# Head pairs in one TensorE visit, and q transposed like k, in a retention and two-MoE kernel

## The chip, the cores and the metric

The kernel runs on one core of a Trainium2 chip. The metric is device time in microseconds, the median of three runs.

## The reference

Three stages follow each other. All inputs are float32; attention has batch 4, 8 heads, 576 tokens and head dimension 64, and the two feed-forward stages see 2304 tokens of 512 features.

```python
scores = scale * np.matmul(q, k.transpose(0, 1, 3, 2))
gamma = 1.0 - 2.0 ** (-5.0 - np.arange(H))
Dmat = np.where(rel >= 0, gamma[:, None, None] ** rel, 0.0)     # rel = i - j
x = np.matmul(scores * Dmat, v)                                 # then (B*S, H*D)
...
h = np.maximum(np.maximum(x @ w1, x @ w2), x @ w3)              # 512 x 768 each
x = h @ w_out                                                   # 768 x 512
...
g = x @ w_gate                                                  # 512 x 1536
out = (g * sigmoid(g) * (x @ w_val)) @ w_out2                   # 1536 x 512
```

## The kernel before

**Attention in chunks.** Heads are taken in pairs, because two heads of 64 fill the 128 partitions, and tokens in halves of 288, each three chunks of 96. A *unit* is one batch, one head pair and one half, so there are 32 units; unit n belongs to pair n // 2, and even units are first halves. Within a chunk the decay mask is applied to the scores; between chunks a running 64x64 state per head carries what came before. For a unit the code has four steps: `a_prep` (k scaled on GpSimd, k and q brought into transposed form, q scaled by powers of gamma), `a_state` (state matmuls on TensorE, then the chain of states on VectorE), `a_score` (score matmuls, then the mask on VectorE into `pT`), and `a_value` (state times q and `pT` times v into one bank, evicted as a high part `xh` and a low part `xl`).

**Two ways to transpose.** For the first PT = 12 units TensorE transposes k against the identity `ident` (L225) and multiplies q by the diagonal tables `dia` (L228), which transposes and scales it in one; GpSimd makes these tables at the start, and ScalarE copies both results out (L230). From unit 12 on, k and q come from HBM as a 32x32-blocked copy `qk` (`t_load`, L188: eight loads of 72 KB for a pair, in runs of 32 floats), and VectorE transposes the blocks.

**The first feed-forward stage is cut into slices.** `f_slice` takes 288 tokens and 128 columns of one of w1, w2, w3: four blocks of 128 rows, each times three matmuls (high times high and two cross terms). The result of w1 is evicted by ScalarE (L362), those of w2 and w3 are joined to it with a maximum on VectorE (L364). Two PSUM banks alternate, so a slice waits for the eviction of the one two before it. Slices of a batch are queued when its four pairs are done and are spread over the later visits.

**Weights.** The 18 weight tiles of that stage, here weights 0 to 17, are 512 KB of 8-byte floats each, loaded on SP's queue (L106; the names `w` and `w64e` are two buffer pools). `conv_steps` brings one to float32 and splits it: two ScalarE steps (L115, L121), VectorE (L123 to L126), a ScalarE copy (L134) and a GpSimd subtraction (L136). When its fourth step is reached, the load of the weight four further on is issued.

**The order.** `tc.manual_schedule` fixes it: every engine and every queue runs its instructions in the order in which the code is written. `visit(n, slices, convs)` writes one unit's part: the value of unit n, loads for later pairs, states and scores of unit n + 1, then `slices` weight slices, with `a_prep(n + 2)` and the steps of `convs` weight conversions spread between them. The main loop (L505) gives visits 0 to 7 no slices, 8 to 13 four, 14 and 15 six, and later ones five. Until slices exist, `spin` matmuls on zeros stand between visits. After the last unit come the rest of the slices and the other two stages.

Of the kernel before, what the change touches and what calls it, by code (L numbers as in the profile page):

```python
# [41 lines left out]
O_E = O_KS + NP * 2  # L42
O_Q = O_E + NP
O_S = O_Q + H
O_M = O_S + H
# [4 lines left out]
def _constants():  # L50

    c = np.zeros((P, NCONST), np.float64)
    gam = 1.0 - 2.0 ** (-5.0 - np.arange(H))
    j = np.arange(CK)
    c[:CK, O_ID:O_KS] = np.eye(CK)
    c[:CK, O_M:O_G] = j[None, :] >= j[:, None]
    for pr in range(NP):
        for e in range(2):
            g = gam[2 * pr + e]
            c[:CK, O_S + 2 * pr + e] = g ** -j / np.sqrt(D)  # L60
            c[64 * e:64 * e + 64, O_G + pr * CK:O_G + (pr + 1) * CK] = g ** j
            c[:CK, O_KS + 2 * pr + e] = g ** (CK - j) / np.sqrt(D)
            c[64 * e:64 * e + 64, O_E + pr] = g ** CK
            c[:CK, O_Q + 2 * pr + e] = g ** j
    return c.astype(np.float32)
# [3 lines left out]
def retention_moe(ctx, tc, consts, q, k, v, w1, w2, w3, w_out, w_gate, w_val, w_out2, out):  # L69
# [3 lines left out]
    def f(ap):  # L73
        return ap.bitcast(F32)
# [11 lines left out]
    psa = psa_cm.__enter__()  # L86

    cst_a = att.tile([P, O_G], F32, name="cst_a", tag="cst_a", bufs=1)
# [3 lines left out]
    e_t = cst_a[:, O_E:O_Q]  # L92
    q_t = cst_a[0:CK, O_Q:O_S]
    s_t = cst_a[0:CK, O_S:O_M]
    mask = cst_a[0:CK, O_M:O_G]
    g_t = cst_g.rearrange("p (r m) -> p r m", r=NP)
    dia = [att.tile([CK, 2, CK], F32, name=f"dia{i}", tag=f"dia{i}", bufs=1) for i in range(NP)]
    d_t = [att.tile([CK, 2, CK], F32, name=f"dm{i}", tag=f"dm{i}", bufs=1) for i in range(NP)]
# [109 lines left out]
    def a_prep(n):  # L208
# [9 lines left out]
        pool.tensor_tensor(u["ks"][:, 0:nk], u["k"][:, 0:nk], sc, ALU.mult)  # L218
        kq = att.tile([P, 2, C], F32, name="kq", tag="kq", bufs=3)
        kt, qg = kq[:, 0], kq[:, 1].rearrange("p (c m) -> p c m", c=NC)  # L220
        g = g_t[:, pr].unsqueeze(1).to_broadcast([P, NC, CK])
        if n < PT:
            tp = psa.tile([P, 2, 512], F32, name="tp", tag="tp")
            for c in range(NC):
                pe.transpose(tp[:, 0, c * CK:(c + 1) * CK], u["k"][:, c].rearrange("p h d -> p (h d)"), ident)  # L225
            for c in range(NC):
# [50 lines left out]
    def a_value(n):  # L277
# [16 lines left out]
        return lambda: dve.tensor_tensor(xl, o, f(xh), ALU.subtract)  # L294


    w_in = {}
# [83 lines left out]

    def visit(n, slices, convs):
        plan = list(conv_plan(convs))
        done = 0

        def share(j):
            nonlocal done
            upto = len(plan) * (j + 1) // (slices + 1)
# [4 lines left out]
            if n >= 16:  # L393
                for _ in range(1 if j % 2 else 2):
                    next(early, None)

        low = a_value(n)
# [8 lines left out]
        a_state(n + 1)  # L406
        low()
        a_score(n + 1)
        for j in range(slices + 1):
            if j == min(2, slices - 1) or not slices:  # L410
                a_prep(n + 2)
            if j or not slices:
                share(j)
            if j < slices:
                f_some(1)

# [57 lines left out]
    a_load(0, "k", 2)  # L474
    a_load(0, "q", 2, act)
    a_load(0, "v")

    def tables(pr):
        for t, sc, src in ((dia, q_t, ident), (d_t, s_t, mask)):
            pool.tensor_tensor(t[pr], src.unsqueeze(1).to_broadcast([CK, 2, CK]),  # L480
                               sc[:, 2 * pr:2 * pr + 2].unsqueeze(2).to_broadcast([CK, 2, CK]), ALU.mult)

# [11 lines left out]
    spin(1)  # L494
    for n in range(NU):
        if n < NP - 1:
            tables(n + 1)
        if 2 <= n < 6:
            win_load(n - 2)
        if n == 5:  # L500
            win_phase(0, 0)
            win_phase(0, 1)
        if n == 9:
            sp.dma_start(out=cst_g, in_=consts[:, O_G:NCONST])
        visit(n, *((0, 0) if n < 5 else (0, 1) if n < 8 else (4, 2) if n < 13 else (4, 3) if n < 14 else (6, 2) if n < 16 else (5, 0)))  # L505
        if n < 8:
            spin(1)
        if n == 15:
            ask(1)
# [412 lines left out]
```

## Time and profile before

| | us |
|---|---|
| runs | 833.75, 836.33, 833.35 |
| median | 833.75 |
| profiled execution | 833.75 |
| its span in the trace | 831.6 |

The page gives, for each engine, its busy time and share of the span, then the span in 40 equal slices of 20.8 us, each digit a busy share in tenths. The granted clock of TensorE stands at its full level in all 40 slices. The timeline gives instructions in order of their start; consecutive ones of the same form are one row with their count, and where an engine had been idle, the row ends with how long and what ended the wait. TensorE's rows overlap, so the distance between two starts is what a piece of work takes there. The list of DMA issues gives the time from issue to landing.

### The profile page before, as it was taken

How to read it: one execution, taken by the hardware profiler on the slowest of the kernel's cores; microseconds unless marked ns; L12 is line 12 of the kernel's file. 1: busy time of each engine (PE TensorE's matmuls, PEld its weight loads, DVE VectorE, ACT ScalarE, POOL GpSimd, SP SyncE). 2: the span in 40 equal slices, each digit the busy share in tenths (PEclk: the TensorE clock that was granted, in tenths of full speed). 3: DMA queues.
4: the chain of work that ended last, by engine and by line, in shares of the span. 5: the costliest groups of instructions: out<-in, count | busy, mean ns of one | idle time of the engine just before them, and what ended most of it. 6: DMA issues, size and time to landing. Idle time of an engine off the chain costs nothing.

```text
span 831.6 us, 15514 instructions
## 1 busy us (share of the span) xinstructions
PE 817.6 (98%) x5933; PEld 762.7 (92%) x5933; DVE 563.4 (68%) x1007; ACT 315.0 (38%) x633; POOL 208.7 (25%) x194
## 2 busy tenths in 40 slices
PE   9999999999999999999999999999999999999998
PEld 6799899998989999999988999999998999999996
DVE  2678857787874354476587888888899455555554
ACT  3554523333321233565445553444443222332220
POOL 4243320000000002342023333233332333222331
PEclk9999999999999999999999999999999999999999
DMA  9999849999981223865555444334420716565522
GB/s 177 230 202 235 174 119 243 254 251 239 253 225 61 81 99 99 247 180 157 198 207 191 146 159 165 143 137 165 161 80 13 266 49 243 216 226 213 204 92 76
DMA packets 165801, 142.94 MB, mean 172 GB/s; under 512 B 101344, under 2 KB 137952, under 8 KB 165728
## 3 DMA queue, kind: packets, MB, share of 16 engines
q1 hardware_dynamic: 164368, 141.56, 57.7%
q8 instruction: 46, 0.75, 0.4%
q10 hardware_dynamic: 1360, 0.41, 0.2%
q14 instruction: 27, 0.22, 0.1%
HBM read 93.70 MB, written 48.23 MB: 171 GB/s over the span
## 4 chain that ended last, share of the span: by engine, by line
PE 68%; issue 14%; DVE 7%; POOL 6%; ACT 2%; DMA 1%; SPq 1%; POOLq 0%; ACTq 0%; DVEq 0%
PE ps L358 26%; PE g L786 17%; PE ps L763 11%; PE ps L715 6%; POOL gl L834 3%; PE s L248 2%; PE o_ps L289 2%; POOL p L807 2%; PE o_ps L285 2%; PE m_ps L264 1%; SPq L188 1%; PE tp L228 1%; PE psz L380 1%; DMA w<-in_moe_w_val_dram 1%; DVE wz L124 0%
## 5 line engine op out<-in xcount | busy, mean ns | idle before, releaser
L358 PE MATMUL ps<-xl,wh 128*128 128x288 f32 x576 | 173.1, 300 | 3.7 <-DVE hmax L364 3.1
L358 PE MATMUL ps<-xh,wh 128*128 128x288 f32 x576 | 169.7, 295 | 0.0
L358 PE MATMUL ps<-xh,wlo 128*128 128x288 f32 x576 | 169.6, 294 | 0.0
L834 POOL TENSOR_TENSOR gl<-p,gh 128x384 fp32r<-128x384 f32 x72 | 85.8, 1209 | 293.7 <-ACT gh L833 293.7
L763 PE MATMUL ps<-wp,gh 128*128 128x512 f32 (+1 forms) x436 | 135.3, 391 | 0.4 <-DVE acc L768 0.3
L358 PEld LDWEIGHTS ps<-xl,wh 128*128 128x128 f32 x576 | 108.0, 188 | 7.6 <-DVE hmax L364 4.0
L358 PEld LDWEIGHTS ps<-xh,wh 128*128 128x128 f32 x576 | 108.1, 188 | 0.0
L358 PEld LDWEIGHTS ps<-xh,wlo 128*128 128x128 f32 x576 | 108.1, 188 | 0.0
L763 PEld LDWEIGHTS ps<-wp,gh 128*128 128x128 f32 x436 | 80.7, 188 | 14.4 <-DVE acc L768 1.0
L364 DVE TENSOR_TENSOR hmax<-ps,hmax 128x288 f32<-128x288 f32 x96 | 43.6, 455 | 68.6 <-PE ps L358 61.9
L763 PE MATMUL ps<-wp,gl 128*128 128x512 f32 (+1 forms) x218 | 85.6, 393 | 0.0
L768 DVE TENSOR_TENSOR acc<-ps,acc 128x512 f32<-128x512 f32 (+1 forms) x91 | 62.2, 684 | 33.6 <-PE ps L763 31.6
L786 PE MATMUL g<-xhB,wa 128*128 128x384 f32 x288 | 73.4, 336 | 0.0
L786 PE MATMUL g<-xhT,wc 128*128 128x384 f32 x288 | 73.2, 335 | 0.0
L546 POOL TENSOR_TENSOR hl<-hf,hh 128x384 fp32r<-128x384 f32 x26 | 30.0, 1163 | 129.3 <-DMA h_d<-hmax 77.4
L833 ACT ACTIVATE gh<-p 128x384 fp32r<-128x384 f32 x72 | 37.8, 525 | 60.4 <-DVE p L837 53.2
L822 ACT ACTIVATE sb<-u 128x384 f32<-128x384 f32 x36 | 18.9, 525 | 110.0 <-DVE u L820 110.0
L218 POOL TENSOR_TENSOR ks<-kn,cst_a 96x384 f32<-96x384 f32 (+1 forms) x32 | 26.3, 825 | 126.1 <-PE m_ps L264 107.6
L786 PEld LDWEIGHTS g<-xhB,wa 128*128 128x128 f32 x288 | 52.1, 188 | 0.0
L786 PEld LDWEIGHTS g<-xhT,wc 128*128 128x128 f32 x288 | 52.0, 188 | 0.0
L814 DVE TENSOR_TENSOR p<-g,p 128x384 f32<-128x384 f32 x36 | 19.9, 554 | 46.4 <-PE g L786 40.6
L362 ACT ACTIVATE hmax<-ps 128x288 f32<-128x288 f32 x48 | 19.7, 410 | 81.4 <-PE ps L358 81.2
(119 smaller groups left out, 1710.9 us busy)
## 6 DMA issues: line engine op xcount, KB each, us to landing
w<-in_moe_w_out_dram SPq DMA_DIRECT2D x18, 512.0 KB, 4.1
w<-l_d SPq DMA_DIRECT2D x28, 256.0 KB, 2.9
h_d<-hmax SPq DMA_DIRECT2D x48, 144.0 KB, 3.3
w<-in_moe_w_dram SPq DMA_DIRECT2D x12, 512.0 KB, 5.9
w<-in_moe_w_gate_dram SPq DMA_DIRECT2D x12, 512.0 KB, 5.8
w<-in_moe_w_val_dram SPq DMA_DIRECT2D x12, 512.0 KB, 6.0
vn<-in_v_dram SPq DMA_DIRECT2D x16, 288.0 KB, 7.6
out_dram<-acc SPq DMA_DIRECT2D x17, 256.0 KB, 2.0
```

Of the source, the lines that this page charges most:

```text
L218: pool.tensor_tensor(u["ks"][:, 0:nk], u["k"][:, 0:nk], sc, ALU.mult)
L358: pe.matmul(ps, l[:, ksl], r, start=n == 0, stop=n == 3 * KD - 1)
L362: act.activation(mx[hb], ps, ACTF.Copy)
L364: dve.tensor_tensor(mx[hb], ps, mx[hb], ALU.max)
L546: (dve if fi in (3, 5) and hx else pool).tensor_tensor(hl, hf, f(hh), ALU.subtract)
L715: pe.matmul(ps[:, 0:HT], l[:, es], rr, start=n == 0, stop=n == 3 * F1 - 1)
L763: pe.matmul(ps[:, cs], l[:, sl], r[:, cs], start=n == 0, stop=n == 3 * GRP - 1)
L768: dve.tensor_tensor(a[:, cs], ps[:, cs], a[:, cs], ALU.add)
L786: pe.matmul(ps, l[:, ks], r[:, kc], start=first and n == 0, stop=n == 5, skip_group_check=True)
L814: dve.tensor_tensor(p5, g2, p5, ALU.add)
L833: act.activation(gh[half], t, ACTF.Copy)
L834: pool.tensor_tensor(gl[half], t, f(gh[half]), ALU.subtract)
```

## The change

Units 0 to 11 keep single visits. Their q is now transposed on TensorE with three instructions of the form that k has; ScalarE copies only k, and VectorE multiplies q by the table `g` on its way out of PSUM. The `dia` tables and their constants are gone, and the table `cst_g` is loaded at the start on ScalarE's queue instead of at visit 9 on SP's.

From unit 12 on, a visit takes a pair, both halves at once. `pair_value` makes both values in a two-bank tile, with all state matmuls ahead of all `pT` matmuls. `pair_next` makes the states and then the scores of both halves of the next pair in a four-bank tile, the states in columns that the scores leave free. What VectorE and ScalarE do with them is returned as a list of three pieces, which are written ahead of the next slices. The PSUM pool of the first units is closed and a new one opened in visit 11. Pair 6 gets eight slices with five conversions, pair 7 twelve with four, the others ten. `t_load` for pairs 6 to 9 stands in visits 8 to 11 (before: in every other visit, one pair each), and `visit_pair(6)` calls it for pair 9 once more.

```diff
@@ a_prep
-        kq = att.tile([P, 2, C], F32, name="kq", tag="kq", bufs=3)
+        kq = att.tile([P, 2, C], F32, name="kq", tag="kq", bufs=4)
...
-                pe.transpose(tp[:, 0, c * CK:(c + 1) * CK], u["k"][:, c].rearrange("p h d -> p (h d)"), ident)
-            for c in range(NC):
-                for e in range(2):
-                    pe.matmul(tp[64 * e:64 * e + 64, 1, c * CK:(c + 1) * CK], u["q"][:, c, e],
-                              dia[pr][:, e], start=True, stop=True)
-            act.activation(kq, tp[:, :, 0:C], ACTF.Copy)
+            for i, nm in enumerate("kq"):
+                for c in range(NC):
+                    pe.transpose(tp[:, i, c * CK:(c + 1) * CK], u[nm][:, c].rearrange("p h d -> p (h d)"), ident)
+            act.activation(kt, tp[:, 0, 0:C], ACTF.Copy)
+            dve.tensor_tensor(qg, tp[:, 1, 0:C].rearrange("p (c m) -> p c m", c=NC), g, ALU.mult)
@@ new functions
+    def pair_value(j):
+        o = psa.tile([P, 2, 512], F32, name="o_ps", tag="o2")
+        us = [U.pop(2 * j + h) for h in range(2)]
+        for h, u in enumerate(us):
+            for c in range(1 - h, NC):
+                for e in range(2):
+                    hd = slice(64 * e, 64 * e + 64)
+                    pe.matmul(o[hd, h, c * CK:(c + 1) * CK], u["st"][hd, h * NC + c], u["qg"][hd, c],
+                              start=c == 1 - h, stop=False, skip_group_check=True)
+        for h, u in enumerate(us):
...
+                    pe.matmul(o[64 * e:64 * e + 64, h, c * CK:(c + 1) * CK], u["v"][:, c, e], u["pT"][:, e, c],
+                              start=False, stop=True, skip_group_check=True)
...
+            act.activation(xh, o[:, h, 0:C], ACTF.Copy)
...
+            dve.tensor_tensor(xl, o[:, h, 0:C], f(xh), ALU.subtract)
+    def pair_next(j):
...
+        s = psa.tile([P, 4, 512], F32, name="s", tag="s4")
+        m = [s[:, h, C + c * D:C + (c + 1) * D] for h in range(2) for c in range(NC - h)]
...
+        return [chain_states, lambda: weigh(0), lambda: weigh(1)]
@@ visit
-        else:
-            t_load(n // 2 + 2)
+        if n >= PT - 4:
+            t_load(n - 2)
...
+        if n + 1 < PT:
+            a_score(n + 1)
+            late = []
+        else:
+            swap_banks()
+            late = pair_next(PT // 2)
+        ahead = [n + 2] if n < PT - 2 else [PT, PT + 1] if n < PT - 1 else [PT + 2, PT + 3]
...
+    def visit_pair(j, slices, convs):
+        share = sharing(min(slices, 8 if convs else slices), convs, j >= 8)
+        pair_value(j)
+        share(0)
+        a_load(j + 3)
+        t_load(j + 3)
...
+        late = pair_next(j + 1)
+        for x in range(slices + 1):
+            if late:
+                late.pop(0)()
+            if x in (3, 5):
+                a_prep(2 * j + 4 + (x == 5))
+            if x:
+                share(x)
+            if x < slices:
                 f_some(1)
@@ start and main loop
+    act.dma_start(out=cst_g, in_=consts[:, O_G:NCONST])
...
-    for n in range(NU):
+    for n in range(PT):
...
-        if n == 9:
-            sp.dma_start(out=cst_g, in_=consts[:, O_G:NCONST])
-        visit(n, *((0, 0) if n < 5 else (0, 1) if n < 8 else (4, 2) if n < 13 else (4, 3) if n < 14 else (6, 2) if n < 16 else (5, 0)))
+        visit(n, *((0, 0) if n < 5 else (0, 1) if n < 8 else (4, 2)))
...
+    for j in range(PT // 2, NU // 2):
+        visit_pair(j, *((8, 5) if j == 6 else (12, 4) if j == 7 else (10, 0)))
```

The instructions move at three places. In the rows below a row is an instruction with its line, its output, its input and its shape; names of tiles end in a number that is only theirs. First TensorE, before, from the end of one slice to the start of the next in a first half's visit: the value of this unit (`o_ps`), then states (`m_ps`) and scores (`s`) of the next. An f32 matmul of these forms is two passes in the trace.

```order
L358 MATMUL ps<-xh,wh 128x288
L285 MATMUL o_ps<-kq,st 64x96 x4
L289 MATMUL o_ps<-pT,vn 64x96 x6
L264 MATMUL m_ps<-vn,ks 64x64 x4
L248 MATMUL s<-kq 96x96 x6
L358 MATMUL ps<-xl,wh 128x288
```

TensorE after the change, at a pair's visit, where the states share the tile `s` with the scores:

```order
L417 MATMUL ps<-xh,wh 128x288
L304 MATMUL o_ps<-kq,st 64x96 x10
L309 MATMUL o_ps<-pT,vn 64x96 x12
L332 MATMUL s<-vn,ks 64x64 x10
L339 MATMUL s<-kq 96x96 x12
L417 MATMUL ps<-xl,wh 128x288
```

The same four groups stand between two slices, each as long as those of both halves together, and there are half as many such places. Second, SP's queue before the change, from weight 12 (`w_1116`) over the loads of pair 8 (`kn`, `vn`), weights 13 and 14 (`w64e`) and pair 8's `qk` to weight 15 (`w_1316`); `h_d` is a store of a result:

```order
L106 DMA w_1116<-in_moe_w_dram 128x4x128
L167 DMA kn<-in_k_dram 96x12x64
L167 DMA vn<-in_v_dram 96x12x64
L345 DMA h_d_58<-hmax 128x288
L106 DMA w64e<-in_moe_w_dram 128x4x128 x2
L188 DMA qk<-in_k_dram 32x18x32 x4
L188 DMA qk<-in_q_dram 32x18x32 x4
L106 DMA w_1316<-in_moe_w_dram 128x4x128
```

SP's queue after the change, from the same weight 12 (`w_1100`) to the same weight 15 (`w_1368`):

```order
L108 DMA w_1100<-in_moe_w_dram 128x4x128
L169 DMA kn<-in_k_dram 96x12x64
L169 DMA vn<-in_v_dram 96x12x64
L190 DMA qk<-in_k_dram 32x18x32 x4
L190 DMA qk<-in_q_dram 32x18x32 x4
L404 DMA h_d_58<-hmax 128x288
L108 DMA w64e<-in_moe_w_dram 128x4x128 x2
L169 DMA kn<-in_k_dram 96x12x64
L169 DMA vn<-in_v_dram 96x12x64
L190 DMA qk<-in_k_dram 32x18x32 x4
L190 DMA qk<-in_q_dram 32x18x32 x4
L108 DMA w_1368<-in_moe_w_dram 128x4x128
```

Ahead of weights 13 and 14 a first copy of pair 9's `qk` stands now; pair 8's, which stood behind them, is further up, ahead of weight 11; and ahead of weight 15 stand `kn`, `vn` and the second `qk` of pair 9. Third, ScalarE before the change, where slice 18, the first of weight 9's two, is evicted (the first `hmax`; the second is slice 19). Weight 12 is `w_1116`, weight 13 the first `w64e`:

```order
L115 ACTIVATE wz<-w_1116 128x512
L121 ACTIVATE wl<-w_1116 128x512
L134 ACTIVATE wh<-wl 128x512
L362 ACTIVATE hmax<-ps 128x288
L115 ACTIVATE wz<-w64e 128x512
L362 ACTIVATE hmax<-ps 128x288
L121 ACTIVATE wl<-w64e 128x512
```

ScalarE after the change at the same two weights (`w_1100` is weight 12); the row `hmax` is slice 18:

```order
L117 ACTIVATE wz<-w_1100 128x512
L343 ACTIVATE st<-s 128x64
L123 ACTIVATE wl<-w_1100 128x512
L136 ACTIVATE wh<-wl 128x512
L117 ACTIVATE wz<-w64e 128x512
L123 ACTIVATE wl<-w64e 128x512
L421 ACTIVATE hmax<-ps 128x288
```

The eviction of slice 18 stood ahead of weight 13's first step and now stands behind its first two. In the same way the eviction of slice 24 now stands behind the first two steps of weight 16, the hi copy of weight 15 and the two `xh` copies of pair 7.

## Rows read from the trace of the kernel before

**Rows 1.** The page: busy time by engine; DMA share in 40 slices.

```profile
PE 817.6 (98%) x5933; PEld 762.7 (92%) x5933; DVE 563.4 (68%) x1007; ACT 315.0 (38%) x633; POOL 208.7 (25%) x194
...
DMA  9999849999981223865555444334420716565522
```

**Rows 2.** The page's groups: busy, mean ns of one, idle before and its releaser.

```profile
L358 PE MATMUL ps<-xl,wh 128*128 128x288 f32 x576 | 173.1, 300 | 3.7 <-DVE hmax L364 3.1
...
L364 DVE TENSOR_TENSOR hmax<-ps,hmax 128x288 f32<-128x288 f32 x96 | 43.6, 455 | 68.6 <-PE ps L358 61.9
```

**Rows 3.** Timeline of TensorE, two late visits: start us, us, engine, line, operation.

```profile
149.76 0.30 PE L358 MATMUL ps<-xl,wh 128*128 128x288 f32 x1
...
150.42 0.29 PE L358 MATMUL ps<-xh,wh 128*128 128x288 f32 x1
150.64 0.71 PE L285 MATMUL o_ps<-kq,st 64*64 64x96 f32 x12
151.28 0.72 PE L289 MATMUL o_ps<-pT,vn 96*64 96x96 f32 x12
151.83 0.52 PE L264 MATMUL m_ps<-vn,ks 96*64 96x64 f32 x12
...
152.96 0.40 PE L358 MATMUL ps<-xl,wh 128*128 128x288 f32 x1
153.19 0.29 PE L358 MATMUL ps<-xh,wlo 128*128 128x288 f32 x1
...
161.98 0.55 PE L285 MATMUL o_ps<-kq,st 64*64 64x96 f32 x8
162.45 0.72 PE L289 MATMUL o_ps<-pT,vn 96*64 96x96 f32 x12
163.00 0.40 PE L264 MATMUL m_ps<-vn,ks 96*64 96x64 f32 x8
...
164.01 0.40 PE L358 MATMUL ps<-xl,wh 128*128 128x288 f32 x1
```

**Rows 4.** Timeline of TensorE, the transposes of an early unit.

```profile
15.56 0.47 PE L225 MATMUL tp<-cst_a,kn 96*128 96x96 f32 x3
15.96 0.72 PE L228 MATMUL tp<-dia,qn 96*64 96x96 f32 x12
16.61 0.39 PE L380 MATMUL psz<-zero 128*128 128x512 bf16 x1
```

**Rows 5.** Timeline of SP: issues of weights 10, 11, 13 with 14, 15, 16.

```profile
61.02 0.42 SPq L106 DMA_DIRECT2D w<-in_moe_w_dram  x1
...
69.00 0.43 SPq L106 DMA_DIRECT2D w<-in_moe_w_dram  x1
...
75.47 1.01 SPq L106 DMA_DIRECT2D w64e<-in_moe_w_dram  x2
...
84.46 0.43 SPq L106 DMA_DIRECT2D w<-in_moe_w_dram  x1
...
86.01 0.44 SPq L106 DMA_DIRECT2D w<-in_moe_w_dram  x1
```

**Rows 6.** DMA issues: us to landing, weights 10 and 16; 11 and 15; 13; 14.

```profile
w<-in_moe_w_dram SPq DMA_DIRECT2D x1, 512.0 KB, 5.7
...
w<-in_moe_w_dram SPq DMA_DIRECT2D x1, 512.0 KB, 4.4
...
w64e<-in_moe_w_dram SPq DMA_DIRECT2D x1, 512.0 KB, 4.7
...
w64e<-in_moe_w_dram SPq DMA_DIRECT2D x1, 512.0 KB, 5.9
```

**Rows 7.** Timeline of ScalarE: weight 4's first step, and slice 18's eviction.

```profile
44.09 0.68 ACT L115 ACTIVATE wz<-w64e 128x512 f32<-128x512 f32 x1 [1.14 <-DMA w64e<-in_moe_w_dram]
...
83.90 0.41 ACT L362 ACTIVATE hmax<-ps 128x288 f32<-128x288 f32 x1 [1.46 <-PE ps L358]
```

**Rows 8.** Timeline of TensorE: slice 20's first matmul, and unit 16's value.

```profile
87.70 0.40 PE L358 MATMUL ps<-xl,wh 128*128 128x288 f32 x1
...
119.82 0.55 PE L285 MATMUL o_ps<-kq,st 64*64 64x96 f32 x8
```

More of the change, by code (lines that the diff above doesn't have):

```diff
@@ L42 @@
 O_E = O_KS + NP * 2
-O_Q = O_E + NP
-O_S = O_Q + H
+O_S = O_E + NP
 O_M = O_S + H
@@ L86, in retention_moe, with swap_banks @@
     psa = psa_cm.__enter__()
+    def swap_banks():
+        nonlocal psa_cm, psa
+        psa_cm.__exit__(None, None, None)
+        psa_cm = tc.tile_pool(name="ps_pair", bufs=1, space=PSUM)
+        psa = psa_cm.__enter__()
     cst_a = att.tile([P, O_G], F32, name="cst_a", tag="cst_a", bufs=1)
@@ L294, in a_value @@
         return lambda: dve.tensor_tensor(xl, o, f(xh), ALU.subtract)
+    def pair_value(j):
[8 more added lines that the diff above has]
+        for h, u in enumerate(us):
+            for c in range(NC):
+                for e in range(2):
+                    pe.matmul(o[64 * e:64 * e + 64, h, c * CK:(c + 1) * CK], u["v"][:, c, e], u["pT"][:, e, c],
+                              start=False, stop=True, skip_group_check=True)
+        b, _, pr = units[2 * j]
+        low = []
+        for h in range(2):
+            xh, xl = [ffn.tile([P, C], F32R, name=f"x{x}", tag=f"x{x}{pr}", bufs=4) for x in "hl"]
+            act.activation(xh, o[:, h, 0:C], ACTF.Copy)
+            xs[(2 * b + h, pr)] = (xh, xl)
+            low.append((xh, xl, h))
+        for xh, xl, h in low:
+            dve.tensor_tensor(xl, o[:, h, 0:C], f(xh), ALU.subtract)
@@ new lines, in pair_next, with chain_states, weigh @@
+    def pair_next(j):
+        if j >= NU // 2:
+            return []
+        b, _, pr = units[2 * j]
+        us = [U[2 * j + h] for h in range(2)]
+        s = psa.tile([P, 4, 512], F32, name="s", tag="s4")
+        m = [s[:, h, C + c * D:C + (c + 1) * D] for h in range(2) for c in range(NC - h)]
+        for h, u in enumerate(us):
+            for c in range(NC - h):
+                for e in range(2):
+                    pe.matmul(m[h * NC + c][64 * e:64 * e + 64], u["ks"][:, c, e], u["v"][:, c, e],
+                              start=True, stop=True)
+        for h, u in enumerate(us):
+            for c in range(NC):
+                cs = slice(c * CK, (c + 1) * CK)
+                for e in range(2):
+                    hd = slice(64 * e, 64 * e + 64)
+                    pe.matmul(s[0:CK, 2 * e + h, cs], u["kt"][hd, cs], u["qg"][hd, c], start=True, stop=True)
+        st = att.tile([P, 2 * NC, D], F32, name="st", tag="st", bufs=3)
+        def chain_states():
+            act.activation(st[:, 1], m[0], ACTF.Copy)
+            for g in range(1, 2 * NC - 1):
+                dve.scalar_tensor_tensor(st[:, g + 1], st[:, g], e_t[:, pr:pr + 1], m[g], ALU.mult, ALU.add)
+        def weigh(h):
+            pT = us[h]["pT"] = att.tile([CK, 2, NC, CK], F32, name="pT", tag="pT")
+            dve.tensor_tensor(pT, s[0:CK].rearrange("p (e h) m -> p h e m", h=2)[:, h, :, 0:C].rearrange("p e (c m) -> p e c m", c=NC),
+                              d_t[pr].unsqueeze(2).to_broadcast([CK, 2, NC, CK]), ALU.mult)
+        for u in us:
+            u["st"] = st
+        return [chain_states, lambda: weigh(0), lambda: weigh(1)]
@@ L380, in spin, with sharing @@
             pe.matmul(ps, zero[:, 0:P], zero, start=True, stop=True)
-    def visit(n, slices, convs):
+    def sharing(spread, convs, joins):
         plan = list(conv_plan(convs))
@@ L387, in share @@
             nonlocal done
-            upto = len(plan) * (j + 1) // (slices + 1)
+            upto = len(plan) * (j + 1) // (spread + 1)
             for step in plan[done:upto]:
@@ L392, in share, with visit @@
             done = upto
-            if n >= 16:
+            if joins:
                 for _ in range(1 if j % 2 else 2):
                     next(early, None)
+        return share
+    def visit(n, slices, convs):
+        share = sharing(slices, convs, False)
         low = a_value(n)
@@ L414, in visit @@
             if j < slices:
+                f_some(1)
+    def visit_pair(j, slices, convs):
[4 more added lines that the diff above has]
+        t_load(j + 3)
+        if j % NP == NP - 1:
+            fq.extend((2 * (j // NP) + h, *w) for w in win_units for h in range(2))
+        late = pair_next(j + 1)
+        for x in range(slices + 1):
+            if late:
+                late.pop(0)()
+            if x in (3, 5):
[3 more added lines that the diff above has]
+            if x < slices:
                 f_some(1)
```

21 lines of the change are left out of this document (9 added, 12 removed).

## Prediction

> **What bounds the kernel now.** I read the page's engine line first: TensorE is busy 98% of the span and VectorE 68% [rows 1], so a gain has to be TensorE time. Next come the waits. TensorE's weight-slice matmuls, the largest group, stand idle 3.7 us in the whole run [rows 2]; TensorE hardly waits for anything. Third comes the DMA line of the 40 slices (20.8 us each): the 16 DMA engines are 90% busy or more in the first four slices and 80% in the fifth, and drop to 40% in the sixth [rows 1]. So for the first 100 us or so the loads are as full as TensorE, and what the change does to the order of loads there counts as much as what it takes off TensorE. Its margin is thin: at 44.09 us ScalarE's first step on a weight had waited 1.14 us for that weight's load [rows 7].
>
> The sum is made against the profiled execution, 833.75 us (span 831.6, 2.15 around it), which is also the median of the three runs shown.
>
> **Pairing, on TensorE.** I price one visit of each kind from start to start, because matmuls overlap and their durations don't add up. Five steps between slice matmuls take 0.66 us from 149.76 to 150.42, so 0.132 each and 1.59 for a slice of twelve; where a visit begins or ends, the step is 0.22 (150.42 to 150.64) or 0.23 (152.96 to 153.19), 0.09 and 0.10 more [rows 3]. A second-half visit: 0.09, then 0.64 for state times q (12 passes; an f32 matmul shows as two), 0.55 for weighed scores times v (12), 1.13 for the next states and scores (24), 0.10; together 2.51. A first-half visit: 0.09, 0.47 (8), 0.55 (12), 1.01 (20) and 0.10; 2.22. A pair costs 4.73.
> The price of one more pass in a group is (0.64 - 0.47)/4 = 0.0425, and for the narrower state matmuls (1.13 - 1.01)/4 = 0.03 [rows 3]. So the visit of a whole pair: 0.09; 20 passes, 0.64 + 8 x 0.0425 = 0.98; 24 passes, 0.55 + 12 x 0.0425 = 1.06; states and scores, 1.13 + 8 x 0.03 + 12 x 0.0425 = 1.88; 0.10. That is 4.11, or 0.62 less: four entries into a kind of matmul are paid once instead of twice. Bounds: zero, if an entry's price grows with the group; about 1.0, if all 32 added passes of 96 columns cost 0.03 as the narrow ones do. I take 0.62, since it is the measured step. Eight pairs lie behind the last stall discussed below: 5.0 us.
> State chain, weighing and q's preparation now stand between later slices, and ten or more slices (16 us) lie between a pair's scores and its value: hidden on VectorE, ScalarE and GpSimd.
>
> **Transposes of q, units 0 to 11.** Twelve passes cost 0.65 (15.96 to 16.61); the three transposes of k that stand ahead took 0.40 (15.56 to 15.96) [rows 4]. Three more in the same group cost at least 0.25 by the same table of steps and at most 0.40, so 0.25 to 0.40 is saved per unit, 3.0 to 4.8 in all. I count none of it: in units 0 to 8 TensorE's next real work waits for loads (the wait at 44.09 [rows 7] is on a load), and what is saved in visits 8 to 11, two units' 0.6, falls into the wait below. Added are one VectorE product per unit, of the size of the 0.455 us eviction [rows 2], 5.5 us in all beside TensorE, and cst_g's 192 KB ahead of the first loads; by bytes this is 0.65 us (192/512 of the 1.7 us a weight takes, below), and it is gone from its old place ahead of kn and vn of pair 7. For weight 13 the two cancel.
>
> **The moved loads.** SP's order, shown above, has the qk sets of pairs 7, 8 and 9 earlier by one to two weights, and pair 9's is issued in visit 11 and again in pair visit 6, a duplicate of 576 KB. Two more sets stand ahead of weights 13 to 16, and ahead of 15 and 16 also kn and vn of pair 9.
> What does one cost? Weight 10 was issued at 61.02 and landed 5.7 later, at 66.7; weight 11 at 69.00 + 4.4 = 73.4, with one qk set between [rows 5, 6]. Two weights issued together at 75.47 (1.01 for both, the second half a us after the first) landed at 80.2 and 81.9, so one weight takes 1.7. The set took 6.7 - 1.7 = 5.0. The next set, between weights 14 and 15 (84.46 + 4.4 = 88.9), gives 7.0 - 1.7 = 5.3. I take 5.0, as no gap between sets is left in a queue that is never empty. Bounds: 1.9, a weight's price by bytes; 7.6, SP's whole time from the one issue at 61.02 to that at 69.00, less 0.42 for the weight's own.
> The set is read in runs of 32 floats, 128 bytes. The Trainium skill, page "DMA: Bandwidth & Descriptors", section "Bandwidth", measures 1 MB into 128 partitions at 341 GB/s, which makes an estimated 1.7 us of a set and would give the time of rival B; the same page's "Specifications" ask for at least 512 bytes a run for that rate. The trace (5.0 against 1.7 for a weight) agrees with the second.
>
> Then, with a set at 5.0: weight 13 lands at 80.2 + 10.0 = 90.2. ScalarE's order shown above now has the eviction of slice 18 behind both of this weight's first steps; before, the eviction ran at 83.90 [rows 7] ahead of them. Two steps of 0.68 and an eviction of 0.41 [rows 7] free slice 18's bank at 92.0. With two banks slice 20 waits for that; before, it started at 87.70 [rows 8]. TensorE alone would be there at 87.1, 0.6 earlier from the transposes, so it stalls about 5 us. Next late behind it is slice 26. Weight 14 lands at 91.9; 15 after kn and vn of pair 9 (2.5, between 1.9 by bytes and a set's 5.0) + 5.0 + 1.7 at 101.1; 16 after a store of 144 KB (0.5) and its own 1.7 at 103.3 (before: 86.01 + 5.7 = 91.7 [rows 5, 6]). Slice 24's eviction stands behind three steps of 0.68 and two copies of the eviction's size: 3 x 0.68 + 3 x 0.41 = 3.3, so slice 26 starts at 106.6. TensorE alone: 92.0 + 4 x 1.59 + 4.11 + 2 x 1.59 = 105.6. Ten slices more end at 122.5. Before, the value of unit 16 began at 119.82 [rows 8], after the same 36 slices. The lag of 2.7 has a credit of 1.0: the states and scores of unit 17 are done by then. Remaining lag 1.7, less 5.0 for eight pairs: -3.3, or **830.5 us**.
>
> **Rivals.** *B, the loads come in time.* If a set costs under 2.6 us (weight 13 by 85.4), slice 20 starts at 87.1; 4 + 12 slices and a pair visit end at 87.1 + 16 x 1.59 + 4.11 = 116.7, 3.1 ahead, and with the credit and the pairs 833.75 - 3.1 - 1.0 - 5.0 = 824.7. For it: only two sets were priced, and a weight's 1.7 shows that the engines can go faster. Against: 5.0 and 5.3 agree, in two places where SP issued nothing else large between.
> *D, slower: the sets take their upper price.* With p for a set, weight 16 lands at 81.9 + 2p + (2.5 + p + 1.7) + 2.2 = 88.3 + 3p. At p = 7.6 that is 111.1, slice 26 at 114.4, the end of ten slices at 130.3: lag 10.5, less 1.0, less 5.0, +4.5 or 838.3. It decides from p = 6.1 on (weight 16 at 106.6). For it: SP issues in order, the sets of pairs 8 and 9 reuse two buffers and so wait for VectorE's transposes of units 13 and 15, and weights stand behind them in SP's queue; VectorE is itself held by late weights. Against: VectorE is free 32% of the time.
> *E, grouping gives little.* With no saving per pair, the lag and 0.6 for each of pairs 6 and 7 stay: 833.75 + 1.7 + 0.6 = 836, with half of it 833. For it: the entry prices were worked out from small differences. Against: two group sizes gave the same entries.
>
> **How the numbers follow.** Chances: the forecast 0.46 (p from 4.3 to 5.5 gives 828.4 to 832), B 0.27, D 0.13, E 0.14. The predicted time is the forecast's, 830.5. The range, 824.0 to 837.0, takes in B, E and the lower half of D. Half a per cent, 4.2 us, is about what a measurement can tell from no change: faster means below 829.6. That is B and a fifth of the forecast, 0.36; slower, above 837.9, is half of D, 0.07; the rest, 0.57, within.
>
> **What would show it.** In the trace after: the pair visit at 4.1 us from slice to slice (4.7 refutes the pairing's gain); six transposes a unit at 0.65 to 0.8; eight qk DMAs more than before; weight 13 landing near 90 and slice 20 starting near 92, ScalarE's wait there being a DMA; slice 26 near 106.6; the value of unit 16 near 122.5 against 119.82. If it begins at 117, B holds and the loads were hidden; near 130, D. A time above 834 with weights landing in time would mean that the sum for the pairs is wrong.

## The result, and the profile after

The changed kernel takes 842.57 us (median of seven runs, 836.78 to 844.08) against 835.12 for the kernel before, run with it: a ratio of 1.0089, 95% interval 1.0067 to 1.0111. It is slower by nearly 1%, where 830.5 with a range of 824.0 to 837.0 had been predicted. The profiled execution is one of 841.17 us, span 839.4, so 7.8 us over the span before.

The page after the change, parts 1 and 2 (engine busy times; busy tenths, granted clock and DMA share in 40 slices of 21 us); [rows 1] has the lines before:

```profile
PE 814.4 (97%) x5820; PEld 764.8 (91%) x5825; DVE 568.5 (68%) x1019; ACT 312.6 (37%) x633; POOL 206.4 (25%) x190
...
PE   7998899999999999999998999999999999999998
...
PEclk7998989999999999999999999999999999999999
DMA  9998766999976133666355443344330615655522
```

TensorE is busy 3 us less, and still the span grew. Two lines tell where to look: the first, fourth and sixth slices have a granted clock below full, which no slice had before, and all of them lie in the first 126 us. A stretch table gives the clock as a share of 2.4 GHz (columns: stretch, its length, then busy us of each engine with its instructions, the granted clock, the DMA share and GB/s):

```profile
0.00:20.00 20.00, 14.81 (x103) 10.03 (x106) 4.37 (x10) 3.35 (x7) 6.31 (x14) 0.75 1.16 178
...
60.00:80.00 20.00, 17.43 (x186) 16.26 (x184) 14.00 (x30) 8.55 (x17) 7.76 (x7) 0.87 0.89 173
...
100.00:120.00 20.00, 16.36 (x157) 15.14 (x157) 15.46 (x29) 8.79 (x18) 6.70 (x6) 0.83 0.76 179
...
90.80:110.95 20.15, 15.75 (x98) 14.65 (x96) 18.66 (x33) 8.46 (x16) 6.60 (x7) 0.87 0.93 218
```

And TensorE's waits over the whole span (us in all, times, longest):

```profile
PE s L248 <- DVE kq L230: 3.5, 1, 3.5
PE o_ps L285 <- DVE xl L294: 3.3, 2, 2.0
PE ps L417 <- DVE hmax L423: 3.2, 2, 2.2
...
PE s L332 <- issue: 2.6, 1, 2.6
PE ps L417 <- ACT hmax L421: 1.7, 3, 0.8
```

**Where the time went**, by the starts of the same work in the two timelines. Slice 0 before, slice 0 after, and the value of unit 16 after (before: [rows 8]):

```profile
41.71 0.40 PE L358 MATMUL ps<-xl,wh 128*128 128x288 f32 x1
46.84 0.40 PE L417 MATMUL ps<-xl,wh 128*128 128x288 f32 x1
...
135.25 1.04 PE L304 MATMUL o_ps<-kq,st 64*64 64x96 f32 x20
```

Slice 0 starts at 46.84 instead of 41.71, so 5.1 us are lost in the first visits. By slice 8 the cheaper transposes of two units have won 1.1 back (65.35 against 61.37). Slice 12 is 9.0 late (79.26 against 70.24, with the states and scores of unit 13 done as well, worth 1.0). The value of unit 16 is 15.4 late (135.25 against 119.82, again with 1.0 of credit). From there to the end the changed kernel is faster by 7.6, of which 1.0 is that credit.

The three losses in the timeline. At the start (rows of ScalarE's queue, VectorE and TensorE):

```profile
4.24 0.35 ACTq L570 DMA_DIRECT2D cst_g<-in_consts_dram  x1
...
9.86 0.46 DVE L230 TENSOR_TENSOR kq<-tp,cst_g 128x288 f32<-128x288 f32 x1 [9.86 <-DMA cst_g<-in_consts_dram]
...
5.87 0.98 PE L439 MATMUL psz<-zero 128*128 128x512 bf16 x2
10.38 1.28 PE L248 MATMUL s<-kq 64*96 64x96 f32 x12 [3.52 <-DVE kq L230]
```

The first product of q waits for `cst_g` until 9.86 us, TensorE stands idle for 3.5 us and then works at 1.2 GHz: the twelve passes of the first scores take 1.28 us, where they took 0.75 before. The clock is back at about 20 us. Before:

```profile
7.30 0.75 PE L248 MATMUL s<-kq 64*96 64x96 f32 x12
```

At the change of banks, in visit 11 (VectorE, then TensorE):

```profile
74.64 0.69 DVE L126 SCALAR_TENSOR_TENSOR wz<-w64e,wz 128x512 uint32<-128x512 uint32 x1
75.27 0.46 DVE L294 TENSOR_TENSOR xl<-o_ps,xh 128x288 fp32r<-128x288 f32 x1
...
72.54 0.72 PE L289 MATMUL o_ps<-pT,vn 96*64 96x96 f32 x12
75.83 1.34 PE L332 MATMUL s<-vn,ks 96*64 96x64 f32 x20 [2.56 <-issue]
77.09 2.24 PE L339 MATMUL s<-kq 64*96 64x96 f32 x24
79.26 0.61 PE L417 MATMUL ps<-xl,wh 128*128 128x288 f32 x1
79.67 0.44 PE L417 MATMUL ps<-xh,wlo 128*128 128x288 f32 x1
```

The first matmul in the new banks starts 0.1 us after VectorE has read the last value out of the old ones. The profile names no releaser for it; the same 0.1 us lies between the two in pair_only, g_first, no_dup and pair_conv3 below. That read stands behind conversion steps. TensorE's clock falls to 1.2 GHz within that wait and stays there until about 81.7: 0.24 for a step of a slice instead of 0.13. Slice 12 is 5.0 later against before than slice 8 was; less the credit of 1.0, and with 1.2 more lost inside slice 12, the change of banks costs about 5.2 us.

Third, slices 16 to 23, in pair visit 6: 20.2 us from the first start to the end, where eight slices take 12.7. The last row of the stretch table is that stretch: VectorE is busy 18.66 of 20.15 us there. TensorE waits 4.4 us for evictions in it (0.8, 0.5, 2.2 and 1.0), and behind the wait of 2.2 its clock is at 1.2 GHz, from about 105.6 to the end of the stretch.

The gain is there too. TensorE's timeline at a late pair visit, to be held against [rows 3]:

```profile
236.10 0.29 PE L417 MATMUL ps<-xh,wh 128*128 128x288 f32 x1
236.31 1.04 PE L304 MATMUL o_ps<-kq,st 64*64 64x96 f32 x20
237.29 1.21 PE L309 MATMUL o_ps<-pT,vn 96*64 96x96 f32 x24
238.33 0.75 PE L332 MATMUL s<-vn,ks 96*64 96x64 f32 x20
239.01 1.26 PE L339 MATMUL s<-kq 64*96 64x96 f32 x24
240.20 0.40 PE L417 MATMUL ps<-xl,wh 128*128 128x288 f32 x1
240.44 0.29 PE L417 MATMUL ps<-xh,wlo 128*128 128x288 f32 x1
```

From 236.10 to 240.44 are 4.34 us; less two ordinary steps of 0.13, the pair visit takes 4.08.

### The profile page after: what moved, and what is told of

It reads as the page before. It is cut to its first block, busy times and chain, and to the rows that moved or that the text cites. A ratio compares the mean times of both kernels' runs of the same rounds, so it can differ in the third digit from the quotient of the medians.

```text
span 839.4 us, 15301 instructions
## 1 busy us (share of the span) xinstructions
PE 814.4 (97%) x5820; PEld 764.8 (91%) x5825; DVE 568.5 (68%) x1019; ACT 312.6 (37%) x633; POOL 206.4 (25%) x190
## 4 chain that ended last, share of the span: by engine, by line
PE 64%; issue 15%; DVE 9%; POOL 6%; DMA 3%; ACT 2%; SPq 0%; ACTq 0%; POOLq 0%; DVEq 0%
PE ps L417 24%; PE g L880 16%; PE ps L857 11%; PE ps L809 6%; POOL gl L928 3%; POOL p L901 2%; PE s L339 1%; PE o_ps L309 1%; PE o_ps L304 1%; DVE wz L126 1%; PE s L248 1%; PE o_ps L289 1%; DVE wz L125 1%; PE o_ps L285 1%; DMA w<-in_moe_w_gate_dram 1%
## 5 line engine op out<-in xcount | busy, mean ns | idle before, releaser
L640 POOL TENSOR_TENSOR hl<-hf,hh 128x384 fp32r<-128x384 f32 x26 | 31.8, 1232 | 133.1 <-ACT hh L639 133.1
L916 ACT ACTIVATE sb<-u 128x384 f32<-128x384 f32 x36 | 18.9, 525 | 110.7 <-DVE u L914 110.7
```

The lines of the kernel that those rows point to most:

```text
L640: (dve if fi in (3, 5) and hx else pool).tensor_tensor(hl, hf, f(hh), ALU.subtract)
```

## The experiments

The first theory (theory 1) was three separate costs: the late `cst_g`, the wait at the bank change, and the moved loads, with pair 9's second copy holding SP's queue. Theory 2 was that all of it is lateness of loads. The runs made a theory 3 out of the third cost. Each ratio is against the kernel before, run beside it on the same chip. The last four rows come from another chip than the first eight, so kernels of the two groups are compared by ratios.

| run | median us | ratio, 95% interval |
|---|---|---|
| q_only | 841.92 | 1.0083, 1.0057 to 1.0108 |
| pair_only | 836.61 | 1.0029, 1.0009 to 1.0050 |
| no_dup | 845.04 | 1.0124, 1.0079 to 1.0169 |
| g_first | 840.09 | 1.0078, 1.0047 to 1.0109 |
| conv3 | 839.34 | 1.0063, 1.0036 to 1.0089 |
| swap_slice | 844.30 | 1.0109, 1.0040 to 1.0178 |
| spin_start | 840.80 | 1.0071, 1.0052 to 1.0091 |
| all_fix | 836.53 | 1.0030, 1.0004 to 1.0055 |
| pair16 | 828.30 | 0.9927, 0.9901 to 0.9953 |
| pair_fix | 831.42 | 0.9970, 0.9955 to 0.9984 |
| pair_conv3 | 833.12 | 0.9985, 0.9967 to 1.0002 |
| q_fix | 834.67 | 1.0004, 0.9988 to 1.0019 |

The kernels whose profile has TensorE's clock below full in the first 20 us scatter widely, over 5 to 12 us from run to run, and the mean granted clock explains much of it: the changed kernel's own seven runs span 836.78 us at 0.992 to 844.08 at 0.984. spin_start and q_fix have the same transposes and the full clock there, and each stays within 2.3 us. pair16's four runs lie between 827.36 and 828.99, all at 0.999 or 1.000. Single profiles of the first kind are therefore read by their stretches, not by their totals.

### The two halves of the change apart

**q_only**: the kernel before with the first part.

```diff
-            act.activation(kq, tp[:, :, 0:C], ACTF.Copy)
+            act.activation(kt, tp[:, 0, 0:C], ACTF.Copy)
+            dve.tensor_tensor(qg, tp[:, 1, 0:C].rearrange("p (c m) -> p c m", c=NC), g, ALU.mult)
...
+    act.dma_start(out=cst_g, in_=consts[:, O_G:NCONST])
     a_load(0, "v")
```

> The kernel before with the first part of the change alone: q of units 0 to 11 transposed, scaled on VectorE, cst_g loaded at the start on ScalarE's queue; single visits, loads and slices as before. Theory 1 (the start is a cost of its own): the first q product waits for cst_g until about 9.9 us, TensorE is idle some 4 us, its clock is at 1.2 GHz until about 20 us, slice 0 starts near 46.8 instead of 41.7, and most of these 5 us stay to the end: 837 to 839. Theory 2 (the start is swallowed by later waits for weights, and only the moved loads of the second part cost anything): slice 0 late too, but caught up by visit 16, 833 to 835.

**pair_only**: the changed kernel with that part undone.

```diff
-            act.activation(kt, tp[:, 0, 0:C], ACTF.Copy)
-            dve.tensor_tensor(qg, tp[:, 1, 0:C].rearrange("p (c m) -> p c m", c=NC), g, ALU.mult)
+            act.activation(kq, tp[:, :, 0:C], ACTF.Copy)
...
+        if n == 9:
+            sp.dma_start(out=cst_g, in_=consts[:, O_G:NCONST])
```

> The changed kernel with the first part undone: q by the diagonal tables, ScalarE copies both, cst_g on SP at visit 9; pair visits, moved loads and the duplicate kept (the tables share buffers with the first hmax tiles). Theory 1: slice 0 at 41.7 and the clock full from the start, the wait at the bank swap and the loads' stalls stay: 842.5 less about 5, so 836 to 839. Theory 2: weights 13 and 15 land as late as before relative to SP's holds, nothing gained: 841 to 843.

The first part alone costs 0.8%, the second alone 0.3%. Their sum, 11.6 us, is more than the 7.5 the changed kernel loses; with intervals of 2 us or more to either side this may be overlap or scatter. q_only is slower than either forecast, pair_only is where theory 1 had it. In pair_only slice 0 starts at 42.01 and the clock of the first 60 us is 1.00. In q_only's profile (the fastest of its ten runs) slice 0 starts at 45.93, and the delay stays: the first slice of visit 16 starts at 124.93 against 121.86, and the span ends 3.3 later. Theory 2 falls with that: a late start isn't caught up. Its first stretch is like the changed kernel's:

```profile
0.00:20.00 20.00, 15.29 (x120) 10.35 (x122) 4.37 (x10) 3.25 (x7) 6.32 (x14) 0.74 1.14 178
```

### The start

**g_first**:

```diff
     act.dma_start(out=cst_a, in_=consts[:, 0:O_G])
+    act.dma_start(out=cst_g, in_=consts[:, O_G:NCONST])
...
-    act.dma_start(out=cst_g, in_=consts[:, O_G:NCONST])
```

> The changed kernel with cst_g issued second on ScalarE's queue, ahead of q of the first pair instead of behind it; all else kept. Theory 1: cst_g lands some 4 to 5 us earlier, near 5, q's first product starts near 6.5 to 7, TensorE has no idle stretch over 1.5 us at the start, its clock stays at 2.4 GHz, and slice 0 starts at 42 to 43.5 instead of 46.8; 838 to 840. Rival: with less work per visit TensorE falls to 1.2 GHz in the first 20 us all the same, slice 0 near 45 to 46, 841 to 842.

The first scores start at 7.67, as the theory had it, and slice 0 at 43.31. The clock of the first 20 us is still 0.83: TensorE now waits 1.2 us for q behind the table and 0.6 for the product. So the rival's clock came true, and the theory's start. The total, a ratio of 1.0078 against the changed kernel's 1.0089, is no difference clear of the noise.

**spin_start** keeps the table late and fills the wait with matmuls on zeros.

```diff
-    spin(2)
+    spin(14)
     a_score(0)
```

> The changed kernel with twelve more matmuls on zeros (0.32 us each) between the first transposes and the first scores, where TensorE stands idle from 6.3 to 10.4 us; no other edit, cst_g as late as in the changed kernel. It tells the wait's own price from the clock's. If the fall of the clock costs most: clock full from 6 us on, slice 0 near 43.5 to 45 instead of 46.8, total 839 to 841. If the wait alone costs: slice 0 near 46, total 842.

```profile
0.00:20.00 20.00, 18.04 (x197) 11.62 (x199) 6.40 (x16) 4.71 (x11) 6.89 (x15) 1.00 1.10 170
...
40.00:60.00 20.00, 19.89 (x196) 19.00 (x196) 15.36 (x30) 9.83 (x20) 8.32 (x7) 0.91 1.03 196
```

With the clock kept at 2.4 GHz slice 0 starts at 43.27. So of the 5.1 us lost at the start 1.6 stay with the wait alone, and 3.6 were the clock's. That is so in these two profiles; the same start gave slice 0 at 45.30 in conv3's, 48.49 in no_dup's and 53.41 in swap_slice's, so the clock's part ranges from 2 to 10 us. The clock falls later too, within 40 to 60 us, and the total is 840.8, as forecast for the clock but by its interval not clear of the changed kernel's.

**q_fix**: q_only with g in four pieces and three more matmuls on zeros.

```diff
+    def g_load(i):
+        sp.dma_start(out=g_t[i], in_=consts[:, O_G + i * CK:O_G + i * CK + CK])
     a_load(1)
+    g_load(1)
     a_load(2)
+    g_load(2)
+    g_load(3)
...
-    spin(2)
+    spin(5)
     a_score(0)
```

> The kernel before with q transposed and scaled on VectorE, single visits; g comes in four parts, the first with cst_a, the others on SP behind the loads of pairs 1 and 2, and five instead of two matmuls on zeros cover the first q product. If the first part's only price was cst_g's place: slice 0 near 40.5 to 42, clock full, 831 to 834, no slower than before. If taking TensorE work out of visits that wait for loads makes it idle and its clock fall again between 30 and 50 us: slice 0 later than 42, mean clock under 0.995, 835 to 840.

834.67, between the two forecasts and no different from before, where q_only lost 0.8%: the first part's price was the late `cst_g` and the idle start that it made, which q_fix mends together, and the transposes themselves earn nothing in the total. The stretches show where a gain is lost again:

```profile
20.00:40.00 20.00, 16.15 (x262) 13.25 (x261) 14.94 (x34) 10.08 (x23) 5.47 (x6) 0.95 1.18 230
40.00:60.00 20.00, 20.00 (x180) 19.10 (x182) 13.97 (x28) 9.95 (x21) 7.86 (x6) 0.88 1.14 214
```

Slice 0 starts at 41.12, 0.6 earlier than before. TensorE had been busy 16.2 of the 20 us ahead of 40 (19.0 before), its last wait there, for the eviction `xl`, was 2.0 us, the clock fell, and slices 0 and 1 take 5.1 us instead of 3.3. The same wait of 2.0 us was not followed by a fall in the changed kernel's profile, so what decides it stays open.

### Slices 16 to 23

**no_dup**:

```diff
-        if n >= PT - 4:
+        if PT - 4 <= n < PT - 1:
             t_load(n - 2)
```

> The changed kernel without pair 9's qk loads in visit 11, so that pair visit 6 makes the only ones; all else kept. Theory 1 (SP stands still from 78.5 to 86.7 because these loads wait for VectorE's transposes of unit 15, and weight 13 waits behind): weight 13 is issued near 81 and lands near 86 instead of 96.1; slices 16 to 23 take 13 to 15 us instead of 20.4; 835 to 837. Theory 2 (the queue is full, a set costs its 5 us of transfer): weight 13 lands 5 earlier, at 91, and half of it is seen at the end: 839 to 841.

Both theories are wrong here. Weight 13 comes in time: ScalarE's first step on it had waited for the load in the changed kernel, and doesn't here. The changed kernel, then no_dup:

```profile
96.13 0.67 ACT L117 ACTIVATE wz<-w64e 128x512 f32<-128x512 f32 x1 [0.31 <-DMA w64e<-in_moe_w_dram]
```

```profile
98.02 0.66 ACT L117 ACTIVATE wz<-w64e 128x512 f32<-128x512 f32 x1
```

The stretch of slices 16 to 23 in no_dup:

```profile
93.10:112.05 18.95, 15.31 (x98) 14.18 (x96) 18.33 (x33) 8.42 (x16) 6.49 (x7) 0.91 0.71 154
```

And still the eight slices take 18.9 us, with VectorE busy 18.33 of them. Its total is no better than the changed kernel's; its profile has the clock down once more, within 40 to 60 us (0.83). TensorE's waits for evictions are those of the changed kernel, 0.8, 0.5 and 2.2, but for the last, 0.2 instead of 1.0:

```profile
PE ps L417 <- DVE hmax L423: 2.4, 2, 2.2
...
PE ps L417 <- ACT hmax L421: 1.2, 2, 0.8
```

Of the 7.5 us that these slices lose, 1.2 went with the loads; weight 15, for which ScalarE had waited 3.7 us at their end, is in time as well. The loads aren't what sets the rest. Theory 3: VectorE's work in its written order does. Five conversions of 1.8 us each, the masks and states of two units, two eviction remainders and six transposing steps stand in eight slices, and the evictions that free the slices' banks stand among them.

**conv3**:

```diff
-        visit_pair(j, *((8, 5) if j == 6 else (12, 4) if j == 7 else (10, 0)))
+        visit_pair(j, *((8, 3) if j == 6 else (12, 4) if j == 7 else (10, 0)))
```

> The changed kernel with three weight conversions in pair visit 6 instead of five (pair 7 takes the other two); loads, duplicate, start and swap kept. Theory 3 (the stalls at slices 16 to 23 are VectorE's and ScalarE's work in program order: five conversions, two masks, four states and six transposing steps stand in eight slices, and the evictions stand behind them): slices 16 to 23 take 13 to 15 us instead of 20.0, no fall of the clock there, total 836 to 838. Theory 1 (late weights behind SP's hold): 13 and 15 are still late, the stall moves to the next place that needs them, under 2 us gained, 840 to 842.

```profile
87.00:101.00 14.00, 13.40 (x99) 12.84 (x96) 13.59 (x28) 5.49 (x11) 4.77 (x5) 1.00 0.96 193
```

The loads, the duplicate too, are those of the changed kernel, and the eight slices take 14.0 us at full clock, as theory 3 had it. So the number of conversions between these slices is the third cost. Two things go with a conversion and were not separated from VectorE's own 1.8 us: its steps on ScalarE, and the stretching of VectorE's steps beside GpSimd (last section), which falls from 3.7 us to 1.7. The total, 839.3, is not the 836 to 838 of the forecast; it still has the start in it. With q as before the same edit takes the ratio from 1.0029 (pair_only) to 0.9985 (pair_conv3), 3.7 us less against the kernel before, and its eight slices take 14.0 us too.

### The bank change

**swap_slice**:

```diff
-        else:
-            swap_banks()
-            late = pair_next(PT // 2)
...
         for j in range(slices + 1):
+            if n + 1 == PT and j == 1:
+                swap_banks()
+                late = pair_next(PT // 2)
```

> The changed kernel with one of visit 11's four slices written ahead of the bank swap and of the first pair's states and scores; all else kept. Theory (TensorE waits at the swap for xl of unit 11, 2.8 us, and its clock falls for 5.8 us because of that idle stretch): the wait shrinks to 1.0 to 1.3, the clock stays at 2.4 GHz, slice 16 starts 4 to 5 us earlier; at the end 2 to 4 of it are left: 838.5 to 840.5. Rival (the clock falls for another reason than the wait, or VectorE's work sets the pace there): the wait shrinks but slice 16 starts less than 2 us earlier, 841 to 843.

At the place itself it went as expected: the wait is 0.8 instead of 2.6, and the clock from 60 to 100 us is 1.00. That the shorter wait kept the clock up isn't shown by this, since conv3 has the changed kernel's wait there and kept it too:

```profile
PE s L332 <- issue: 2.6, 1, 2.6
...
60.00:80.00 20.00, 17.42 (x199) 16.38 (x198) 15.93 (x33) 8.71 (x17) 7.79 (x7) 1.00 0.76 179
```

The total, 844.30 instead of 838.5 to 840.5, says nothing of the place. In the profiled run the clock stayed low until past 30 us and fell again after 40; slice 0 started at 53.41. Such a start hides any gain behind it, so the later runs were made on the old start.

**pair_conv3** and **pair_fix**: pair visits from unit 12 on with q as before, three conversions in pair visit 6, and pair_fix also with the slice ahead of the change and without the duplicate.

```diff
-        visit_pair(j, *((8, 5) if j == 6 else (12, 4) if j == 7 else (10, 0)))
+        visit_pair(j, *((8, 3) if j == 6 else (12, 4) if j == 7 else (10, 0)))
...
+            if n + 1 == PT and j == 1:
+                swap_banks()
+                late = pair_next(PT // 2)
```

> Pair visits from unit 12 on, q of the first units as before, three conversions in pair visit 6; swap and duplicate as in the changed kernel. Beside the run with q as before and five conversions (836.6) it prices the fifth and fourth conversion, beside the next one up the swap and the duplicate. Theory 3 (VectorE's order sets slices 16 to 23): 5 us less, 830 to 833. Theory 1 (late loads): 835 to 837.

> Pair visits from unit 12 on as in the changed kernel, q of the first units as before, and three edits: one slice ahead of the swap, three conversions in pair visit 6, no duplicate. If the start was the first part's only price and the other two costs are mended: slice 0 at 42, value of pair 8 near 119 to 121, clock full throughout, 826 to 829. If crowding VectorE into pair visits costs in any spread: 831 to 834.

TensorE's wait at the change of banks, in pair_conv3 and then in pair_fix:

```profile
PE s L338 <- issue: 4.5, 1, 4.5
```

```profile
PE s L338 <- issue: 0.8, 1, 0.8
```

833.12 and 831.42: the slice and the missing duplicate give 1.7 us together, hardly clear of the noise, with 3.7 less wait at the change in the profiles. Which of the two edits gave how much was not separated. pair_fix misses the 826 to 829 of a mended kernel and lies in the 831 to 834 forecast for VectorE's crowding; slices 16 to 23 still take 15.6 us in it, VectorE busy in 14.2 of them, where eight slices without a wait take 12.7.

### All edits, and the pairing by itself

**all_fix**: the changed kernel with g's first columns beside `cst_a`, and the edits of swap_slice, conv3 and no_dup.

> The changed kernel with all four edits: the first pair's 96 columns of g loaded with cst_a (the rest behind, on the same queue), one slice ahead of the bank swap, three conversions in pair visit 6, no duplicate. If the start, the swap and VectorE's crowded pair visit are the costs and the pair visits save 0.62 each: slice 0 near 41.7 to 42.5, value of pair 8 near 117 to 119, total 824 to 828. If something else holds the changed kernel back: above 830.

836.53, far from 824 to 828: the edits help (a ratio of 1.0030 for 1.0089), but the clock is down again, 0.74 in the first 20 us and 0.77 from 40 to 60, and slice 0 starts at 46.31. Of its ten runs the fastest, 830.74, is the one with a mean clock of 0.998.

**pair16**: the kernel before up to unit 15, then pair visits.

```diff
-    for n in range(PT):
+    for n in range(16):
...
-    for j in range(PT // 2, NU // 2):
-        visit_pair(j, *((8, 5) if j == 6 else (12, 4) if j == 7 else (10, 0)))
+    for j in range(8, NU // 2):
+        visit_pair(j, 10, 0)
```

> The kernel before up to unit 15 (tables, single visits, loads and conversions as before, tables sharing buffers with the first hmax tiles), and pair visits with ten slices from unit 16 on, where no weight of the first stage is converted; one slice ahead of the bank swap. It measures the pairing by itself. Theory (the pair visit saves 0.62 to 0.8 us a pair, the losses of the changed kernel all lie before unit 16): 828 to 830, about 5 us faster. Rival (a pair visit saves little, the changed kernel's gain behind unit 16 came from elsewhere): 832 to 835.

828.30, a ratio of 0.9927, and the fastest kernel here. Its page:

```profile
PE 811.1 (98%) x5925; PEld 761.1 (92%) x5933; DVE 562.5 (68%) x1007; ACT 314.9 (38%) x633; POOL 207.9 (25%) x194
...
PEclk9999999999999999999999999999999999999999
```

Eight pairs save 5.7 us against the kernel before run with it (833.96), 0.71 each. By the two profiles the value of unit 16 begins at 121.92 against 119.82, of which 1.0 is work done ahead, and the end comes 4.6 earlier: 5.7 are gained behind it and about 1 is lost before. Here no weight of the first stage is converted between the slices of a pair visit.

## Why the prediction was wrong, point by point

**The pair visit was priced right.** 4.11 was worked out, 4.08 measured; 5.0 for eight pairs was worked out, 5.7 measured by pair16. By the timeline a pair saves 4.73 less 4.08, 0.65, or 5.2 for eight. Behind 140 us TensorE's waits for VectorE's evictions are 1.9 us before, 1.3 in pair16 and none in the changed kernel, which would make up the rest in the profiles of both; no run separates it.

**The transposes gain nothing, as said, but their start was mis-priced.** The step "by bytes this is 0.65 us" took `cst_g` as a share of a queue. What counted is that the first product of q needs it: it was issued at 4.24 and used at 9.86, and the scores that follow stood 3 us later than before (10.38 against 7.30). The prediction had the transposed q ready when k is, and never asked when its new operand lands. The saving was sized too small besides: between slices the six transposes of a unit take 0.44 us (50.13 to 50.57) where k's three and q's twelve passes took 0.99 (45.00 to 45.99). That saves 0.55, where the sum had 0.25 to 0.40.

**The clock was left out.** No term of the sum had TensorE at its lower level, since the page before shows none. It fell to 1.2 GHz after three waits of 2.2 to 3.5 us in the changed kernel, and in other kernels here from some point between 38 and 48 us, mostly behind two waits of 1.3 and 1.8 to 2.0 us for `xl`. It did not fall each time: not behind 2.6 us at the bank change of conv3, not behind 3.0 us in spin_start's pair visit 6. At the start it cost 3.6 of 5.1 us, by the two profiles compared. The sum counted time taken from TensorE in a stage that waits for loads as worth nothing; in q_fix's profile the 0.6 us won by slice 0 are followed by 1.8 lost at half clock in the next two slices.

**The bank change was counted at nothing.** The section on the change says that a new pool is opened in visit 11, and the prediction gives that no price. The new pool's first matmul waits for the last reader of the old one, on an engine (VectorE) whose order puts conversion steps ahead. It cost 2.6 us idle and, with some 6 us at half clock, 5.2 in all.

**The moved loads: the mechanism of rival D was there, and it wasn't the cause.** SP did stand still, for 6.2 us in one wait, for VectorE's transposes of unit 15, with weight 13 behind it, which landed at 96.1 rather than the predicted 90.2. But no_dup took that away and the slices stayed slow. The first stall is at slice 20, behind the eviction of slice 18 and both first steps of weight 13, as forecast; but it is 0.8 us and not 5, and ScalarE came late to these steps because the copy ahead of them had waited 3.2 us for VectorE's part of weight 12, in no_dup as well. Nor is a set's price traced to its short runs, as the prediction has it: SP alone takes 4.1 us to issue the eight loads (86.71 to 90.82), and the DMA engines are 0.78 busy from 88 to 90; no run tells the two apart.

**VectorE was cleared by a mean.** State chain, weighing and q's preparation were put down as "hidden on VectorE, ScalarE and GpSimd", at nothing, and "VectorE is free 32% of the time" is the span's share [rows 1]. In pair visit 6 it is busy 93% (18.66 of 20.15 us). The order rows ahead of the prediction showed which steps an eviction on ScalarE stands behind; the same count on VectorE, five conversions at 1.8 us and the masks, states and transposes of two units against eight slices of 1.59 us, would have shown it too. It was the step that failed for the largest loss: 7.5 us in eight slices, 6.2 of which went when two conversions did.

The sign was given 0.07. Rival D, which stood for slower, put its turning point on the landing of a weight; the true one was the number of conversions between slices.

## What to carry to other kernels

An engine's share over the span says nothing about a stage: where work is moved closer together, count every in-order engine's work there against the stage's length. A constant that a changed formula needs is priced by when it lands against its first use, not by its bytes. And time taken from TensorE in a stretch that waits for something else need not be neutral: waits of 2 to 4.5 us were often, not always, followed here by half clock that cost about as much again, so a gain is better tried first where nothing else is tight, as pair16 does.

## What the hardware showed beyond that

Some steps of VectorE took about three times as long, or nearly twice, while GpSimd worked. Timelines of the changed kernel, VectorE and then GpSimd:

```profile
96.11 1.36 DVE L125 TENSOR_SCALAR wz<-wz 128x512 uint32<-128x512 uint32 x1
97.51 1.20 DVE L126 SCALAR_TENSOR_TENSOR wz<-w,wz 128x512 uint32<-128x512 uint32 x1
...
100.32 1.56 DVE L235 TENSOR_TENSOR kq<-qt,cst_g 128x288 f32<-128x288 f32 x1
```

```profile
95.90 1.29 POOL L138 TENSOR_TENSOR wlo<-wl,wh 128x512 fp32r<-128x512 f32 x1 [4.66 <-PE ps L417]
97.15 1.00 POOL L220 TENSOR_TENSOR ks<-kn,cst_a 96x384 f32<-96x384 f32 x1
100.28 1.29 POOL L138 TENSOR_TENSOR wlo<-wl,wh 128x512 fp32r<-128x512 f32 x1 [2.12 <-ACT wh L136]
```

Elsewhere the same steps take 0.42, 0.69 and 0.46 us; each of these three began while a GpSimd operation ran, and ended 0.3 to 0.6 us after it (GpSimd's spans in the profile are rough). Not every step is stretched: a transposing step (L233) at 85.86, beside a GpSimd operation from 84.86 to 86.15, took its usual 0.47. The Trainium skill, page "SBUF — State Buffer", section "Terms", says that the two engines share a port pair which one holds for a whole instruction while the other is blocked; the trace agrees as far as the overlap goes, and no run here took GpSimd's work away to prove it. In pair visit 6 five steps are stretched in this way, by 3.7 us together.

The other surprise is how far the clock of one program varies: the changed kernel ran between 836.8 and 844.1 us with mean clocks of 0.992 to 0.982, and a kernel with the clock full in every slice, pair16, repeats within 1.7 us in its four runs.
